# Moving the 64-row output jobs behind all wide jobs, with ten repeated transposes more, in an attention-plus-spectral-mix kernel

## The chip, the core and the metric

The kernel runs on one core of a Trainium2 chip. The metric is the device time of one execution in microseconds; a figure quoted for a kernel is the median of its runs. Spans and times inside a span come from the profile, whose zero is the first counted work; a span is some 2 us shorter than the timed run.

## The reference, cut to what matters

```python
def _attn_ref(q, k, v, f):                     # B, H, S, D = 8, 8, 576, 64
    scores = scale * q @ k^T + (cum[i] - cum[j])   # cum = cumsum(log f), causal
    return softmax(scores) @ v

def _moe_ref(x, w_r, w_i, w_ch):               # x: (8, 576, 512), 64 modes
    X = np.fft.rfft(x, axis=1)
    Y[:, :64] = einsum(X[:, :64], w_r + i w_i)     # one 512x512 matrix per mode
    u = x + np.fft.irfft(Y, n=S, axis=1)
    return u + np.maximum(u @ w_ch, 0.0)       # out: (8, 576, 512) float32
```

The output has 8 x 576 x 512 x 4 bytes = 9.44 MB. 576 rows are four blocks of 128 and one of 64 for each of the 8 batches; the 64-row blocks are what the change moves.

## The kernel before

Attention and transforms run while GpSimd's queue loads q, k, v and 64 + 64 weight matrices. After the last weights a tail is left, in which each job makes up to 256 rows of output: TensorE sums `u` and `z` (two PSUM tiles), ScalarE copies `u`, VectorE computes `max(z, 0) + u`, and SyncE issues the write. The list of jobs before:

```python
jobs = []
for b in range(0, B, 2):
    if b == 0:
        jobs += [((c, sb), (c, sb + 1)) for c in (b, b + 1) for sb in (0, 2)]
    else:
        jobs += [((b, sb), (b + 1, sb)) for sb in range(4)]     # wide jobs
    jobs.append(((b, 4),))                                      # a 64-row job: two batches
```

Sixteen jobs make 256 rows each: twelve of them, called wide, take 128 rows from each of two batches, and the four of batches 0 and 1 take 256 rows of one. Four are 64-row jobs. The writes:

```python
def emit_o(job, ps, u, o, pair, split=False):
    ...
        nc.vector.scalar_tensor_tensor(
            o[:, bs, :], ps[1][:, bs, :], 0.0, u[:, bs, :], ALU.max, ALU.add
        )
        if sb == 4:                      # 64 rows of batch b and 64 of batch b + 1
            for h in range(2):
                nc.sync.dma_start(
                    out[b + h, 512:576, :], o[64 * h : 64 * h + 64, 0, :]
                )
        ...
        elif sb % 2 or n_wide < 2:       # a pair of wide jobs: two writes of 512 KB
            ...                          # (the first two wide jobs are written singly)
                nc.sync.dma_start(
                    out[bj, 128 * (sb - sb % 2) :, :][0:256, :].rearrange(
                        "(p r) e -> p r e", r=2
                    )[:, rs, :],
                    pair[:, j, rs, :],
                )
```

The repeated transposes are in the attention stage. They do no useful work; they only add instructions:

```python
VREP = range(16, 25)
...
for sc in [0] * (5 if s in VREP else 0) + list(range(NSB)):
    nc.tensor.transpose(vp[:, sc, :, :]..., VTs[...][:, h, sc * 128 : (sc + 1) * 128], ident_bf)
```

The softmax here doesn't subtract the row's maximum and nothing guards it: scores larger than these inputs give would overflow.

## Time and profile before

| | before |
|---|---|
| time | 436.08 us, median of 3 (436.05 to 436.23) |
| span of the profile | 434.3 us |
| last weights land, last weight matmuls | 399.3, 399.38 us |
| output arithmetic of VectorE | 403.1 to 426.2 us |
| last output packet | 432.6 us |
| last block of TensorE instructions fetched | 425.1 us, 0.92 us on one DMA engine |

Two tools go below the printed lines. The first is a table by windows: for each stretch of the span, the busy time of every engine, the granted TensorE clock, the busy share of the 16 DMA engines and GB/s. The second is the trace's packet records, read by a script, as no view prints them: every DMA packet with its start, duration, size and queue, but not the DMA engine that carried it. Below, *tail* means the time from the start of the last weight matmul to the end of the span: 434.28 - 399.57 = 34.7 us here.

### The profile page before, as it was taken

To read this page: it belongs to the slowest core of one execution; us is meant where nothing else is said; L and a number is where in the kernel's file an instruction comes from. 1 tells how busy PE (TensorE), PEld (TensorE's weight loads), DVE (VectorE), ACT (ScalarE), POOL (GpSimd) and SP (SyncE) were. 2 spreads that over 40 slices of the span, in tenths; PEclk is the share of its full clock that TensorE was granted. 3 is DMA by queue.
4 is the path that set the end of the run, shared out by engine and by line. 5 is a ranking of instruction groups with operands and counts; after the bars stand their busy time and mean duration, and the time that the engine had idled before them with its cause. 6 is when DMAs were issued, how large, how long until landed. Compare 5 with 4: busy or idle time off the path is not lost.

```text
span 434.3 us, 12369 instructions
## 1 busy us (share of the span) xinstructions
PE 358.8 (83%) x5328; PEld 247.5 (57%) x5346; DVE 264.4 (61%) x659; ACT 225.0 (52%) x339; POOL 126.8 (29%) x198
## 2 busy tenths in 40 slices
PE   3787799999987978878778797799999977888881
PEld 2454566776665756666656565666665544554540
DVE  5797888876465665556566577524324654653892
ACT  2888488774526446364464554143443443731771
POOL 8333332223232232332323322232222322200400
PEclk9996899996557868577597779599999999999997
DMA  8999999999999999999999999999999999996697
GB/s 181 235 235 239 236 237 238 246 212 217 228 220 237 220 229 233 215 237 227 222 236 212 213 211 211 211 211 211 211 211 211 211 211 211 211 212 127 240 383 272
DMA packets 51086, 97.39 MB, mean 224 GB/s; under 512 B 3799, under 2 KB 12983, under 8 KB 51031
## 3 DMA queue, kind: packets, MB, share of 16 engines
q0 software_dynamic: 46464, 85.65, 101.0%
q1 hardware_dynamic: 4567, 10.95, 7.1%
q8 instruction: 42, 0.69, 0.6%
q14 instruction: 13, 0.11, 0.1%
HBM read 163.73 MB, written 9.44 MB: 399 GB/s over the span
## 4 chain that ended last, share of the span: by engine, by line
PE 33%; DMA 27%; ACT 11%; DVE 11%; issue 5%; DVEq 0%; POOL 0%; ACTq 0%; SPq 0%
DMA wb<-in_moe_w_i_dram 26%; ACT E L590 8%; PE pav L628 7%; PE A L191 6%; PE ps L583 6%; PE tp L321 5%; PE vp L555 3%; PE px L671 2%; DVE QTs L336 2%; ACT KT L334 2%; DVE x_all L650 1%; DVE os L1019 1%; PE pz L842 1%; DVE XT L685 1%; DVE E L605 1%
## 5 line engine op out<-in xcount | busy, mean ns | idle before, releaser
L590 ACT ACTIVATE E<-ps 128x1024 bf16<-128x1024 f32 (+1 forms) x128 | 101.3, 849 | 28.2 <-PE pav L628 17.2
L191 PE MATMUL A<-XT,wb 128*128 128x16 bf16 x1984 | 71.9, 181 | 12.0 <-DMA wb<-in_moe_w_i_dram 7.0
L191 PEld LDWEIGHTS <-wb 128*128 128x128 bf16 x1984 | 64.1, 100 | 27.5 <-issue 13.2
L96 POOL DMA_DIRECT2D wb<-in_moe_w_r_dram x64 | 42.7, 667 | 123.6 <-PE A L191 24.7
L583 PE MATMUL ps<-QTs,KT 64*128 64x64 bf16 (+4 forms) x384 | 55.8, 320 | 14.5 <-ACT E L590 12.4
L96 POOL DMA_DIRECT2D wb<-in_moe_w_i_dram x64 | 42.3, 660 | 81.7 <-DMA wb<-in_moe_w_i_dram 38.1
L628 PE MATMUL pav<-va,E 128*128 128x65 bf16 (+1 forms) x1088 | 53.6, 205 | 7.1 <-DVE x_all L650 6.5
L628 PEld LDWEIGHTS <-E 128*128 128x128 bf16 (+1 forms) x1088 | 43.6, 111 | 17.2 <-DVE x_all L650 8.9
L605 DVE TENSOR_TENSOR E<-E,trimask 128x256 bf16<-128x256 bf16 (+2 forms) x128 | 37.0, 304 | 19.5 <-ACT E L590 18.8
L881 ACT CAST XW<-pxw 128x512 bf16<-128x512 f32 x36 | 20.7, 587 | 35.6 <-PE pxw L874 23.4
L340 ACT COPY VT<-tp 128x640 bf16<-128x640 bf16 (+1 forms) x32 | 23.1, 759 | 28.3 <-PE tp L321 28.3
L583 PEld LDWEIGHTS <-KT 64*128 64x128 bf16 x384 | 19.1, 99 | 31.4 <-issue 20.8
L334 ACT COPY KT<-tp 128x640 bf16<-128x640 bf16 (+1 forms) x32 | 22.0, 751 | 26.0 <-PE tp L321 25.8
L924 ACT CAST XW<-pB 128x512 bf16<-128x512 f32 x36 | 21.1, 586 | 26.7 <-PE pB L842 26.6
L874 PE MATMUL pxw<-wch,yy 128*128 128x512 bf16 x133 | 33.6, 385 | 1.1 <-issue 0.5
L923 DVE CAST x_all<-pA 128x512 bf16<-128x512 f32 x36 | 24.9, 692 | 12.5 <-PE pA L842 10.6
L336 DVE COPY QTs<-tp 128x640 bf16<-128x640 bf16 (+1 forms) x32 | 23.4, 768 | 14.2 <-PE tp L321 14.0
L650 DVE TENSOR_TENSOR x_all<-pav,rcp 128x384 bf16<-128x384 f32 x64 | 29.1, 455 | 1.1
L639 DVE RECIPROCAL rcp<-pav 128x6 f32<-128x6 f32 x64 | 12.1, 189 | 24.5 <-PE pav L628 23.6
L156 DVE TENSOR_TENSOR YTe<-A,Yacc 128x128 bf16<-128x128 f32 x16 | 5.9, 368 | 33.1 <-PE A L191 33.1
L555 PE MATMUL vp<-ident_bf,VT 128*128 128x128 bf16 x205 | 21.4, 256 | 4.5 <-DVE QTs L336 3.8
L842 PEld LDWEIGHTS <-ident_bf 64*64 64x64 bf16 (+1 forms) x336 | 15.1, 107 | 17.0 <-issue 8.2
(142 smaller groups left out, 610.8 us busy)
## 6 DMA issues: line engine op xcount, KB each, us to landing
wb<-in_moe_w_r_dram POOLq DMA_DIRECT2D x62, 512.0 KB, 16.7
wb<-in_moe_w_i_dram POOLq DMA_DIRECT2D x62, 512.0 KB, 17.4
stv<-in_v_dram POOLq DMA_DIRECT2D x9, 576.0 KB, 15.6
out_dram<-os SPq DMA_DIRECT2D x10, 512.0 KB, 4.8
stk<-in_k_dram POOLq DMA_DIRECT2D x11, 288.0 KB, 15.6
stq<-in_q_dram POOLq DMA_DIRECT2D x11, 288.0 KB, 15.4
wx<-in_v_dram POOLq DMA_DIRECT2D x5, 576.0 KB, 16.2
out_dram<-uo SPq DMA_DIRECT2D x3, 512.0 KB, 4.2
```

The source lines that it names most:

```text
L96: keep(nc.gpsimd.dma_start(dst, src))
L191: ins = nc.tensor.matmul(A[:, eb, mi, :], lhsT=w_of(mi, eb * 128), rhs=x_of(m), start=(i == 0), stop=(i == len(terms) - 1),)
L334: nc.scalar.copy(rows(KTs[pr % 2][:, :, 0:S]), tv)
L336: ins = nc.vector.tensor_copy(rows(QT[pr][:, :, :]), tv)
L555: nc.tensor.transpose(vp[:, sc, :, :].rearrange("p b d -> p (b d)"), VTs[s // 2 % 2][:, h, sc * 128 : (sc + 1) * 128], ident_bf[:, :],)
L583: nc.tensor.matmul(ps[:, b, o : o + n], lhsT=KTs[pr % 2][bs, h, jb * 128 : (jb + 1) * 128], rhs=QT[pr][bs, h, jb * 128 + c0 : jb * 128 + c ...
L590: nc.scalar.activation(E[:, :, piece * 512 : piece * 512 + w], ps[:, :, 0:w], ACT.Exp, scale=scale,)
L605: nc.vector.tensor_tensor(dg, dg, tr, ALU.mult)
L628: nc.tensor.matmul(pav[64 * half : 64 * half + w, slot, :], lhsT=E[:, b, c : c + (w - 1) * st + 1 : st], rhs=va[:, jb, b, :], start=(n == ...
L650: nc.vector.tensor_tensor(xo, pi, ri, ALU.mult)
L874: nc.tensor.matmul(pxw[:, :], lhsT=xT[:, eb, i * 128 : (i + 1) * 128], rhs=wch[:, eb, :], start=(eb == 0), stop=(eb == NDC - 1),)
L923: nc.vector.tensor_copy(xs, pA[:, :])
```

## The change

The intent: 64-row jobs no longer stand between wide jobs but follow them all, and ten more transposes in the attention stage move the points at which TensorE fetches its instructions.

```diff
-    VREP = range(16, 25)
+    VREP = range(16, 27)
...
                 jobs += [((b, sb), (b + 1, sb)) for sb in range(4)]
-            jobs.append(((b, 4),))
+        jobs += [((b, 4),) for b in range(0, B, 2)]
```

## The prediction

> **What bounds the kernel now.** I read the page first, then the chain of waits in order of time, then a table of the last 35 us by windows, then SyncE's own queue. The page says how the DMA engines stand over the whole span (40 slices of 10.86 us) and what the queues carried:
>
> ```profile
> span 434.3 us, 12369 instructions
> ...
> DMA  8999999999999999999999999999999999996697
> ...
> q0 software_dynamic: 46464, 85.65, 101.0%
> q1 hardware_dynamic: 4567, 10.95, 7.1%
> q8 instruction: 42, 0.69, 0.6%
> ```
>
> From the second slice to the 36th the DMA row shows 9: the loads of q, k, v and the weights are one unbroken stream. No TensorE work of that stage sets the end unless it starves the stream. The median weight load takes 16.7 us from issue to landing (part 6 of the page), so some 16 us of transfers stand queued at any time. The chain in order of time shows where the stream ends and the tail begins:
>
> ```profile
> 384.11 15.23 DMA wb<-in_moe_w_i_dram
> ...
> 414.97 1.24 DVE os L1019
> ...
> 416.29 3.23 DMA out_dram<-uo
> ...
> 425.18 0.41 DVE os L1019
> ```
>
> The last weights land at 399.3. All that the reordering touches lies behind it: 434.3 - 399.3 = 35.0 us. Windows of that tail (time, then busy us of PE, PEld, DVE, ACT and POOL, granted clock, DMA share, GB/s):
>
> ```profile
> 408.60:412.90 4.30, 3.84 (x64) 2.18 (x67) 3.91 (x4) 3.00 (x4) 0.00 (x0) 1.00 0.93 332
> 412.90:418.60 5.70, 4.78 (x78) 2.72 (x74) 5.31 (x6) 4.44 (x5) 0.00 (x0) 1.00 1.00 369
> 418.60:424.30 5.70, 4.78 (x74) 2.51 (x67) 5.31 (x6) 4.44 (x5) 0.00 (x0) 1.00 1.02 393
> 424.30:427.50 3.20, 0.75 (x6) 0.13 (x3) 1.88 (x3) 0.59 (x1) 0.00 (x0) 1.00 0.99 361
> 427.50:430.10 2.60, 0.00 (x0) 0.00 (x0) 0.00 (x0) 0.00 (x0) 0.00 (x0) 0.74 1.02 410
> 430.10:434.30 4.20, 0.00 (x0) 0.00 (x0) 0.00 (x0) 0.00 (x0) 0.00 (x0) 0.50 0.34 102
> ```
>
> Two things are nearly equal here. VectorE is busy 5.31 of the 5.70 us of a group (four wide jobs and one 64-row job). The DMA share is 1.00 from 412.9 on and stays there for 4 us after the last arithmetic (426.2). So the output DMA, not VectorE, has the last word. SyncE's issues at the end:
>
> ```profile
> 421.26 2.54 SPq L1026 DMA_DIRECT2D out_dram<-uo  x2
> 423.90 3.52 SPq L1039 DMA_DIRECT2D out_dram<-os  x4
> 427.54 2.48 SPq L1026 DMA_DIRECT2D out_dram<-uo  x2
> ```
>
> The two writes of a 64-row job (128 KB each) hold the queue 2.5 us; four writes of wide jobs (512 KB each) hold it 3.5 us. The last arithmetic ends at 426.2, its writes start issuing only at 427.5 and finish issuing at 430.0; the data flows until about 432.
>
> **What the Trainium skill says.** "DMA: Bandwidth & Descriptors", section "The descriptor swizzle", gives partitions 0-63 to the even SBUF ports and 64-127 to the odd ones. A 64-row write reads from one half only, so half of the ports can serve it. The trace agrees in part: its packet records show 2 KB packets of 64-row writes taking 113 to 136 ns in the windows in which they dominate against 85 to 86 ns for the 2 KB packets of wide writes, and the rate falls from 410 GB/s to 186-268 GB/s around 411.5, 418.3, 424.3 and 430.5. "Perfetto Trace Analysis", section "Per-instruction lifecycle", says that the profiled time of such an issue is lock wait and descriptor generation, without the movement. The trace shows one and the same kind of issue at 0.33 to 1.18 us (wide) and 0.54 to 1.48 us (64 rows), which I read as waiting for room behind earlier writes. "Runtime: NRT & Kernel Launch", section "Instruction fetch mechanics", has instructions fetched in blocks of 16 KiB, 256 instructions each. Queue 8 agrees: 42 packets, 0.69 MB, 16,384 bytes each, 0.9 to 1.0 us on one of the 16 DMA engines. The last ones start at 393.3, 401.3, 413.4 and 425.1.
>
> **The change part by part.**
>
> *Ten more transposes.* Two more attention steps repeat five transposes each. A run of ten such transposes lasts 1.22 us in the chain where a run of five lasts 0.69, so five more cost 0.53 us, ten 1.06 us of TensorE, around 165 to 180 us. The weight queue is some 16 us deep, so the load stream does not notice: 0 us on the end. They put 20 instructions (ten weight loads, ten matmuls) ahead of everything later. Each fetch comes 20 instructions earlier in the program, at some 0.05 us an instruction in the tail about a microsecond. The fetch of 401.3 would start near 400.4, still behind the last weights. That of 425.1 would start about 424. A fetch costs its engine about 0.9 us while the others go on, which fits the straggling packets after 431.75 (1.5 us with under a tenth of the engines busy). Moving it earlier does not remove it: 0 to -0.4 us.
>
> *Three 64-row jobs leave the gaps between wide jobs.* VectorE: each 64-row job takes 0.68 us, and two gaps of about 0.2 us stand around it (the waits for ScalarE's copy and "issue"). Without them the wide jobs follow each other at about 1.13 us, the spacing that three in 3.48 us show. Twelve wide jobs from 408.7 then end near 422.4 in place of 424.2-425.6, and the four 64-row jobs at 0.8 to 0.9 us each end near 425.8, against 426.2. Gain 0.4 us, but not at the end, as writes are behind.
>
> *Writes.* All 9.44 MB are the same. From 407.75, when the engines are first full, some 8.69 MB remain (9.44 less 0.75 that the packet records show before). Of these 6.59 MB go as 4 KB packets at 410 GB/s, 16.1 us; 1.05 MB as 2 KB packets of the first two wide jobs at 370 GB/s, 2.8 us; 1.05 MB as 64-row writes. In the kernel before, a 64-row job costs 0.26 MB / 410 = 0.64 us plus a loss of about 0.42 us, read from the two windows with dips (453 and 433 KB moved in 1.5 us where 615 would have been): 1.06 us, four of them 4.2 us. The sum is 23.1 us, so 430.9, and the records show the bulk ending about 431.5; the rest is the starving around 411-412 (rate 186 GB/s, share 0.71), where the first 64-row job held SyncE. The change removes that: the first wide write can be issued near 410 in place of 411.28. Gain 0.3 to 0.6 us.
>
> *What is given back.* Behind all wide jobs four 64-row jobs write alone, with no wide packets to fill the other half of the ports. At about 215 GB/s, 1.05 MB take 4.9 us in place of 4.2: +0.6.
>
> Sum: -0.45 (starving) -0.2 (VectorE, straggler; mostly hidden) +0.6 (half the ports) -0.4 (the last write to wait for is 128 KB, and no 1 MB pair stands in front of it) = about -0.45 us. 436.08 becomes 435.6.
>
> **The rivals.** (1) *SyncE becomes the bound.* If the 2.5 us for two 64-row writes is their own cost, not waiting for room, the four jobs take 4 x 2.5 = 10 us from about 423.6, so 433.6 for the last issue against 430.0: +3 us, 439. For it: every 64-row pair took over 2 us, whatever came before. Against it: the first write of the first job took 0.54 us, and wide issues also stretch to 1.18 us. I give it one in ten. (2) *Latency-bound 64-row writes.* If only about three writes may be outstanding, each 128 KB, and each needs about 2.2 us, the last megabyte runs at 175 GB/s and takes 6 us: +1 us net, 437. One in five. (3) *Full rate.* If writes of the two halves overlap, all 64-row data go near 400 GB/s and the end comes at about 434.7. One in five. (4) *The fetch shift disturbs the stream*: a fetch that falls before 399.3 would delay one engine's weights by 0.9 us, 436.8. The fetch has about a microsecond of room; one in ten.
>
> **Range and chances.** The middle is -0.45 us; rival 3 sets the lower edge at 434.6, rivals 2 and 4 the upper at 437.0, rival 1 lies outside. 2% is 8.7 us, a quarter of the whole tail, beyond any of these: faster 0.01, same 0.98, slower 0.01.
>
> **What would show it.** The last weights should land at 399.3 within 0.3 us. VectorE's wide jobs should run unbroken, 1.13 us apart, ending by 422.5. The dip in the output rate near 411-412 should be gone, and one long stretch near 215 GB/s should stand at the end. 64-row issues should shorten to about 0.6 us once the wide writes have drained; if they stay at 1.0 to 1.5 us with the engines idle, rival 1 is right and I am wrong. If the last weights land later, the fetch part is wrong.

## The result

435.81 us (435.36 to 436.12, six runs) against 436.06 us for the kernel before in the same rounds (435.78 to 436.84). The ratio is 0.9991, 95% interval 0.9978 to 1.0004: same, within the predicted range, and by itself not clear of noise. In a later set of rounds the changed kernel had 435.58 against 436.47, ratio 0.9982 (0.9970 to 0.9995).

The page of the changed kernel, the rows that answer to those shown of before:

```profile
span 434.1 us, 12383 instructions
...
DMA  8999999999999999999999999999999999996798
...
q1 hardware_dynamic: 4567, 10.95, 7.2%
q8 instruction: 42, 0.69, 0.6%
```

The stream of loads is as full as before. The same number of blocks is fetched. The tail by windows, with the same columns as in the prediction (time, busy us of PE, PEld, DVE, ACT, POOL, clock, DMA share, GB/s):

```profile
408.60:413.50 4.90, 4.19 (x67) 2.13 (x64) 4.88 (x5) 4.05 (x4) 0.00 (x0) 1.00 1.02 391
413.50:414.50 1.00, 0.93 (x20) 0.53 (x16) 1.00 (x2) 0.89 (x1) 0.00 (x0) 1.00 0.55 201
414.50:422.80 8.30, 7.77 (x108) 3.58 (x104) 8.30 (x9) 7.38 (x9) 0.00 (x0) 1.00 1.03 406
422.80:427.30 4.50, 1.85 (x18) 0.64 (x15) 2.55 (x4) 1.17 (x2) 0.00 (x0) 0.91 1.02 403
427.30:432.30 5.00, 0.00 (x0) 0.00 (x0) 0.00 (x0) 0.00 (x0) 0.00 (x0) 0.50 0.91 223
432.30:434.10 1.80, 0.00 (x0) 0.00 (x0) 0.00 (x0) 0.00 (x0) 0.00 (x0) 0.50 0.03 7
```

The three dips around 64-row writes are gone from the middle. VectorE is busy all the time up to 422.8. At the end stands one stretch of 5.0 us at 223 GB/s, in which only 64-row writes move, and it ends sharply. But a hole of one microsecond at 201 GB/s is there at 413.5. VectorE's wide jobs and SyncE's issues, from the timeline (start, length, engine, line, instruction, count):

```profile
408.86 13.91 DVE L1019 SCALAR_TENSOR_TENSOR os<-pz,us 128x1024 f32<-128x1024 f32 x12
...
410.10 14.59 SPq L1039 DMA_DIRECT2D out_dram<-os  x14
424.79 6.25 SPq L1026 DMA_DIRECT2D out_dram<-uo  x8
427.26 3.77 SPq L1026 DMA_DIRECT2D out_dram<-uo  x6
```

Twelve wide jobs take 13.91 us, 1.16 us each, without a gap. The eight 64-row writes are issued in 6.25 us; the last six of them, issued once the wide data had mostly drained, take 3.77 us, 0.63 us each with the gaps, where each pair of before took 2.1 to 2.5 us. The chain of waits, in order of time, differs in one place ahead of the tail:

```profile
383.85 0.91 PE A L191 x30
...
399.88 0.29 PE A L175 x8
...
424.99 0.69 DVE uo L1019
```

From 383.85 to the last weight matmuls it is TensorE that holds the path, not the loads: those matmuls come at 399.8, 0.43 us later than before (399.38), although the packet records put the last weight packet at 398.6, against 398.8 before. The reason is in the granted clock between 384 and 390 us (changed kernel, then the kernel before):

```profile
384.00:390.00 6.00, 5.95 (x61) 3.00 (x60) 2.81 (x5) 1.76 (x3) 0.53 (x1) 0.72 1.12 211
```

```profile
384.00:390.00 6.00, 5.86 (x97) 3.76 (x98) 3.03 (x6) 2.35 (x4) 0.53 (x1) 1.00 1.12 211
```

At a clock of 0.72 TensorE did 61 recorded matmuls where it did 97 before. So of the tail's gain, 34.7 - 34.1 = 0.65 us, this profile gave 0.43 us away again before the tail began. Whether that belongs to the change was the first thing to test.

### The profile page after: what moved, and what is told of

It reads as the page before. It is cut to its first block, busy times and chain, and to the rows that moved or that the text cites. A ratio compares the mean times of both kernels' runs of the same rounds, so it can differ in the third digit from the quotient of the medians.

```text
span 434.1 us, 12383 instructions
## 1 busy us (share of the span) xinstructions
PE 360.6 (83%) x5338; PEld 249.1 (57%) x5356; DVE 263.5 (61%) x659; ACT 225.5 (52%) x339; POOL 126.9 (29%) x198
## 4 chain that ended last, share of the span: by engine, by line
DMA 36%; PE 30%; ACT 9%; DVE 8%; issue 4%; POOL 0%; ACTq 0%; DVEq 0%
DMA wb<-in_moe_w_i_dram 36%; ACT E L590 7%; PE pav L628 6%; PE A L191 5%; PE tp L321 5%; PE ps L583 4%; PE vp L555 2%; PE pu L842 2%; DVE QTs L336 2%; ACT KT L334 2%; PE px L671 1%; PE pz L842 1%; DVE os L1019 1%; DVE x_all L650 1%; DVE E L605 1%
## 5 line engine op out<-in xcount | busy, mean ns | idle before, releaser
L583 PE MATMUL ps<-QTs,KT 64*128 64x64 bf16 (+4 forms) x384 | 53.7, 312 | 14.6 <-ACT E L590 12.4
L881 ACT CAST XW<-pxw 128x512 bf16<-128x512 f32 x36 | 20.7, 587 | 34.8 <-PE pxw L874 23.4
L340 ACT COPY VT<-tp 128x640 bf16<-128x640 bf16 (+1 forms) x32 | 23.3, 759 | 28.8 <-PE tp L321 28.7
L924 ACT CAST XW<-pB 128x512 bf16<-128x512 f32 x36 | 20.9, 586 | 29.8 <-PE pB L842 29.7
L874 PE MATMUL pxw<-wch,yy 128*128 128x512 bf16 x133 | 32.9, 379 | 1.1 <-issue 0.5
```

What stands on the lines that cost most here:

```text
L583: nc.tensor.matmul(ps[:, b, o : o + n], lhsT=KTs[pr % 2][bs, h, jb * 128 : (jb + 1) * 128], rhs=QT[pr][bs, h, jb * 128 + c0 : jb * 128 + c ...
L874: nc.tensor.matmul(pxw[:, :], lhsT=xT[:, eb, i * 128 : (i + 1) * 128], rhs=wch[:, eb, :], start=(eb == 0), stop=(eb == NDC - 1),)
```

## The experiments

Twelve runs were made, three of them repeats (e3, e9, e13); each has five timed executions, e7 four. A table first; the tail is read from each run's own profile. Rows between lines shared a chip and the runs of the kernel before.

| run | time us | before us | ratio (95%) | tail us |
|---|---|---|---|---|
| before, first profile | 436.08 | | | 34.7 |
| changed kernel, first | 435.81 | 436.06 | 0.9991 (0.9978 to 1.0004) | 34.1 |
| --- | | | | |
| e1 reordering only | 435.79 | 436.47 | 0.9989 (0.9976 to 1.0003) | 34.0 |
| e2 transposes only | 435.93 | 436.47 | 0.9989 (0.9976 to 1.0001) | 33.9 |
| e3 changed kernel again | 435.58 | 436.47 | 0.9982 (0.9970 to 0.9995) | 34.0 |
| e4 second half on ScalarE's queue | 436.03 | 436.47 | 0.9992 (0.9980 to 1.0005) | 34.4 |
| --- | | | | |
| e6 one write, wrong rows | 434.73 | 436.20 | 0.9965 (0.9953 to 0.9978) | 32.9 |
| e7 one write from GpSimd | 442.78 | 436.20 | 1.0152 (1.0138 to 1.0165) | 41.5 |
| e8 ten transposes fewer | 437.08 | 436.20 | 1.0022 (1.0008 to 1.0035) | 35.0 |
| e9 before again | 436.49 | 436.20 | 1.0008 (0.9996 to 1.0021) | 34.8 |
| --- | | | | |
| e10 interleaved rows | 434.94 | 436.25 | 0.9965 (0.9952 to 0.9979) | 33.1 |
| e11 the same, old order | 435.02 | 436.25 | 0.9974 (0.9958 to 0.9991) | 33.4 |
| --- | | | | |
| e12 interleaved, 20 instructions fewer | 435.39 | 436.87 | 0.9964 (0.9951 to 0.9976) | 33.2 |
| e13 e10 again | 435.07 | 436.87 | 0.9958 (0.9944 to 0.9971) | 33.0 |

The tail, from one profile a run, repeats much better than the time: 34.7 and 34.8 for the kernel before, 34.1 and 34.0 for the changed one, 33.1 and 33.0 for e10 and e13, while single runs of one kernel spread over a microsecond. Differences under half a microsecond are therefore read from tails.

My theory going in was that the reordering makes the gain in the stream of writes, and that the transposes do nearly nothing. The rival was the reverse.

### e1: the reordering alone

```diff
-    VREP = range(16, 27)
+    VREP = range(16, 25)        # in the changed kernel
```

> The reordering alone, with nine steps of repeated transposes as before. Theory A (the gain is made by the write stream behind the last weights): time 0.2 to 0.6 us under the kernel before; the tail from the last weight matmuls to the end about 33.9 us as in the changed kernel (34.6 before); VectorE's twelve wide jobs unbroken, about 13.9 us; 64-row stretch near 215 GB/s at the end. Rival B (the ten transposes and the shifted fetches make the gain): time equal to before within 0.15 us, or slower, and packets straggling at the end as before. Rival C (only the granted clock differs between profiles): no difference in the tail either.

Measured: tail 34.0 us, as in the changed kernel; 435.79 against 436.47. The reordering by itself is enough for the shorter tail. The clock between 384 and 390 us was 0.72 again and the last weight matmuls came at 399.8 again, here without the transposes.

### e2: the transposes alone

```diff
-    VREP = range(16, 25)
+    VREP = range(16, 27)        # in the kernel before
```

> The ten transposes alone, jobs in the order of before. Theory A: within 0.15 us of before, the last weights land at about the same time, the tail 34.6 us as before, with the same three dips of the output rate around the 64-row writes. Rival B: 0.2 to 0.6 us faster, and the straggling packets at the end gone. A slowing of 0.3 us or more would say that the longer attention stage reaches the end after all.

Measured: a miss for my theory. In the old order the ten transposes alone shorten the tail to 33.9 us, and the time is 435.93 against 436.47. The dips of the output rate are as before. VectorE's arithmetic keeps its place (from first to last 23.06 us, before 23.04); only the data ends sooner after it started: the last output packet comes 28.7 us after the first output arithmetic, 29.5 in the kernel before. What differs most plainly is the last fetch of instructions: at 423.1 us in place of 425.1. It is not alone: the fetch before it moved too (413.4 to 412.2), and with 2 MB still to write e2 is already 0.3 us ahead, counted from the first output arithmetic (22.95 us, before 23.25). Each part alone gives 0.7 to 0.8 us of tail, and together they give 0.65: the two gains do not add.

### e3: the changed kernel again

> The changed kernel once more, to have it in the same rounds as its two parts. Theory A: equal to the reordering alone within 0.2 us, 0.2 to 0.6 us under before. Its profile may or may not show the low granted clock of 0.72 at 384 to 390 us that the first profile of it showed; if the clock is 1.00 there, the last weight matmuls should come near 399.4 as before (they came at 399.9) and the span fall by up to 0.4 us. Rival: the late last weight matmuls belong to the change itself and come again at 399.9 with the clock at 1.00.

Measured: 435.58 us, tail 34.0. This time the clock stayed at 1.00 between 384 and 390, and the last weight matmuls came at 399.03:

```profile
384.00:390.00 6.00, 5.89 (x90) 3.59 (x89) 3.14 (x6) 2.34 (x4) 0.36 (x1) 1.00 1.13 212
```

The rival is refuted: the late weight matmuls of the first profile are not a property of the change. The span was 433.3 us here. This clock can explain a part of the spread between runs, not all of it: in e2 it was 1.00, and the last weights themselves landed late (the last matmuls waited for them until 399.79).

### e4: the two halves side by side

```diff
-    nc.sync.dma_start(
+    (nc.sync, nc.scalar)[h].dma_start(
         out[b + h, 512:576, :], o[64 * h : 64 * h + 64, 0, :]
```

> The changed kernel, but the second of the two 128 KB writes of each 64-row job is issued from ScalarE's queue, so that rows from partitions 0-63 and 64-127 move side by side. Theory (each write alone can use only one half of the SBUF ports): the last megabyte moves at 350 to 400 GB/s in place of 215, the packets of 2 KB take 85 to 100 ns in place of 131 to 147, and the end comes 1 to 2 us earlier than in the changed kernel: ratio to before near 0.995. Rival (64-row writes are slow for another reason: their own size, or the receiving memory): still 200 to 250 GB/s, and the time within 0.3 us of the changed kernel. Rival 2: ScalarE waits in its queue behind VectorE before each write and holds up the copies of the following 64-row jobs; then the arithmetic ends later than 425.7 and the gain shrinks.

Measured: 436.03 us, tail 34.4: no gain. The rates show why (windows of e4, the last two are after most of the arithmetic):

```profile
421.00:425.50 4.50, 3.78 (x40) 1.32 (x30) 3.79 (x5) 2.79 (x5) 0.00 (x0) 1.00 1.03 401
425.50:427.50 2.00, 0.00 (x0) 0.00 (x0) 0.69 (x1) 0.19 (x1) 0.00 (x0) 1.00 1.01 315
427.50:432.00 4.50, 0.00 (x0) 0.00 (x0) 0.00 (x0) 0.00 (x0) 0.00 (x0) 0.74 0.92 306
```

Side by side the end runs at 306 GB/s in place of 223. Wide packets are in this window until 429.9; from 430 to 431, with 64-row packets of both queues alone, it is 309 GB/s, and a 2 KB packet takes 95 ns on average in place of 135. But the writes from partitions 64-127 no longer wait behind the wide writes; they run beside them and slow those to 315 GB/s from 425.5 on. The low rate begins two microseconds sooner and is less deep. The last packet comes 28.7 us after the first output arithmetic (28.8 in the changed kernel), but the span ends 2.17 us after it (1.71): the extra 0.4 us of tail lies behind the data. The second rival came true too: ScalarE's last copy was held up and the arithmetic ended at 426.4 instead of 425.7. The run speaks for a limit in each half, as its writes still have 128 KB each, but the rate stayed under the 350 GB/s that I had expected.

### e6: one write from all partitions

```diff
-    for h in range(2):
-        nc.sync.dma_start(
-            out[b + h, 512:576, :], o[64 * h : 64 * h + 64, 0, :]
-        )
+    one = out[b, 512, :]
+    nc.sync.dma_start(
+        bass.AP(tensor=one.tensor, offset=one.offset,
+                ap=[[D, 64], [S * D, 2], [1, D]]),
+        o[:, 0, :],
+    )
```

> The changed kernel with one write of 256 KB per 64-row job in place of two of 128 KB: all 128 partitions at once, row r of the two batches taken from partitions 2r and 2r+1. The values land in wrong rows on purpose; bytes, target region and arithmetic are the same. Theory (half of the SBUF ports limits a 64-row write): the last megabyte moves at 370 to 410 GB/s in place of 215 (packets of 2 KB at 85 to 95 ns in place of 131 to 147), it takes some 2.7 us in place of 5, and the tail from the last weight matmuls to the end falls from 34.0 to about 31.8 to 32.5 us, 1.5 us or more off the time. Rival (the small contiguous target region or the packet size is slow): still 215 to 250 GB/s and a tail of 34 us.

Measured: 434.73 us against 436.20, tail 32.9 (wrong rows). The window in which the 64-row data moves:

```profile
427.60:430.20 2.60, 0.00 (x0) 0.00 (x0) 0.00 (x0) 0.00 (x0) 0.00 (x0) 0.87 1.02 386
430.20:433.00 2.80, 0.00 (x0) 0.00 (x0) 0.00 (x0) 0.00 (x0) 0.00 (x0) 0.50 0.08 31
```

386 GB/s against 223, with the same bytes in packets of the same 2 KB to the same target regions. A packet takes 86 ns on average in place of 135. The rival (small packets, or the region in memory) is refuted: what made the 64-row writes slow is that each read from one half of the partitions. One write of 256 KB instead of two of 128 KB was part of the edit, so the size of a write was not separated here; against it as the cause stand the 309 GB/s and 95 ns of e4, whose writes have 128 KB. The issues, at 0.5 to 0.8 us each once the wide data had drained, were not the limit in either case. The tail stayed 0.4 us above what I had expected, because a few packets trail behind the bulk (the second line); more on these under e8 and e9.

### e7: one write in the right rows, from GpSimd

```diff
+    nc.gpsimd.dma_start(
+        bass.AP(tensor=one.tensor, offset=one.offset,
+                ap=[[S * D, 2], [D, 64], [1, D]]),
+        o[:, 0, :],
+    )
```

> The changed kernel with one write of 256 KB per 64-row job from all 128 partitions, issued from GpSimd's queue, rows where they belong (correct result). If that write is spread over all 16 engines by partition, the last megabyte moves at 350 GB/s or more and the tail falls by 1 to 2 us as in the run with wrong rows. If it is spread over few engines because the outer dimension of the target is 2, the rate falls far under 215 GB/s and the time rises by several us.

Measured: 442.78 us, the second case of the expectation. The windows after the wide writes:

```profile
428.00:434.00 6.00, 0.00 (x0) 0.00 (x0) 0.00 (x0) 0.00 (x0) 0.00 (x0) 0.50 0.52 124
434.00:441.20 7.20, 0.00 (x0) 0.00 (x0) 0.00 (x0) 0.00 (x0) 0.00 (x0) 0.50 0.17 45
```

A share of 0.17 of 16 engines is fewer than three. I put this down to the target's outer dimension of 2, where e6 has 64 outside and 2 inside. That is argued, not separated: the edit also changed the queue, and with it the packets (4 KB, with many of 8 bytes between them, in place of 2 KB). GpSimd's queue as such can keep the engines busy: the weight loads on it have a share of 1.12.

### e8 and e9: ten transposes fewer, and the kernel before again

```diff
-    VREP = range(16, 25)
+    VREP = range(16, 23)        # e8, in the kernel before; e9 has no edit
```

> The order of before with ten repeated transposes fewer than before, 20 instructions, so that the last block of instructions, fetched at 425.1 in before while the last writes move, begins behind the program's end or later. Theory (that fetch holds one DMA engine 0.9 us, and its late packets set the end of the kernel before): if the fetch is gone, the tail is 33.9 to 34.1 us as with ten transposes more, and 0.3 to 0.7 us of the time go; if it comes later instead, at 426 or after, the stragglers are as in before or worse, 34.7 us or more. Rival (ten transposes more helped in another way, or the difference was noise of single profiles): 34.7 us as before although the fetch is gone.

> The kernel before once more, to see what its profile repeats. Theory: fetch near 425.1 again, a few late packets after the bulk of the output again, and 34.6 to 34.8 us from the last weight matmuls to the end; time equal to before within 0.2 us. If the tail comes out at 34.0 us, the difference of the tails that I read between single profiles is not to be trusted.

Measured: e9 repeats the kernel before (tail 34.8, last fetch at 425.3). In e8 the fetch did not vanish; it came later, at 426.0, and the tail is 35.0 us, the second case of the expectation. The time, 437.08 against 436.20, is clearly slower, the only such case among the runs that differ in transposes alone. Not all of that is the tail: the clock of this profile was 0.72 between 384 and 390 us again, and the last weight matmuls came at 399.7. The same window of one microsecond, 431.5 to 432.5, for before, e2 and e8:

```profile
431.50:432.50 1.00, 0.00 (x0) 0.00 (x0) 0.00 (x0) 0.00 (x0) 0.00 (x0) 0.50 0.14 51
```

```profile
431.50:432.50 1.00, 0.00 (x0) 0.00 (x0) 0.00 (x0) 0.00 (x0) 0.00 (x0) 0.50 0.11 39
```

```profile
431.50:432.50 1.00, 0.00 (x0) 0.00 (x0) 0.00 (x0) 0.00 (x0) 0.00 (x0) 0.50 0.48 164
```

In these spans output arithmetic began at 403.1 (before), 403.5 (e2) and 403.5 (e8), so e2 is further along at the same distance from its start. Counted from that beginning, the last packet comes 29.5 us later in before, 29.6 in e9, 28.7 in e2 and 29.7 in e8, with the last fetch at 425.1, 425.3, 423.1 and 426.0.

This is the pattern that I take from it. A fetch holds one DMA engine (0.9 to 1.3 us for the last one, up to 1.8 us for earlier ones in the tail) and leaves its share of the writes late. A late engine can catch up while all the others are held back by a 64-row write. In e2 the fetch falls just ahead of the third dip (424 to 425.5); in before, e9 and e8 it falls as that dip ends or behind it, and only wide writes and one last 64-row job follow. In the new order every fetch of the tail has the 5 us stretch at 223 GB/s (the slow stretch) behind it, so there its place does not matter: the last packets come 28.8 us after the first output arithmetic in e1 (fetch at 425.1), in the changed kernel (422.7) and in e3 (421.9).

How much of this is shown can be read from the end of the packet records: the time from the first output arithmetic until 50 KB are left to write, and the time that these last 50 KB take.

| run | until 50 KB are left, us | the last 50 KB, us |
|---|---|---|
| before, e9 | 28.5, 28.7 | 1.1, 0.9 |
| changed kernel, e1, e3 | 28.6, 28.6, 28.7 | 0.3, 0.2, 0.2 |
| e6, e10, e13 (new order, no slow stretch) | 26.8, 26.8, 26.7 | 1.2, 1.4, 1.4 |
| e2, e8 (old order, transposes changed) | 28.0, 28.5 | 0.8, 1.3 |

In before mostly one or two packets are in flight while the last 50 KB move. Up to there the changed kernel is not ahead of before; its whole gain lies in the last 50 KB. Where the slow stretch is taken away (e6, e10, e13), the trailing packets are back. So it is shown that the slow stretch at the end hides packets that otherwise trail. That the last fetch makes them trail fits, but is inferred: the records do not name the engine, and e11 (below), with no fetch after 414.4, still takes 0.8 us for its last 50 KB. In the old order the trailing packets account for 0.3 of the 0.8 us of e2. In e8 they account for most of the 0.3 us lost, but there VectorE's arithmetic also ran 0.5 us longer (23.6 us), as TensorE waited until 405.0 for a copy of `yy`. With one profile each and other fetches moved as well, the effect of the last fetch's place is suggested by e2 and e8, not shown.

### e10 and e11: the right rows, in both orders

e6 can be made correct: the matmuls can put row r of batch b + k on partition 2r + k. Two permuted unit matrices and two scattered basis tables (in the space of a table that is no longer needed) take the place of 64x64 blocks, and a job has four matmuls of 128x128 instead of eight of 64x64.

```diff
+    perm = [BI[:, 128 * t : 128 * t + 128] for t in range(2)]
+    BIp = [BI[:, 256 + 128 * t : 384 + 128 * t] for t in range(2)]
+    for t in range(2):
+        nc.vector.memset(BIp[t][:, :], 0.0)
+        for k in range(2):
+            hf = k ^ t
+            nc.vector.tensor_copy(
+                _strided(perm[t][:, k : k + 1], [[2, HM]]), ident_bf[:, HS[hf]])
+            nc.vector.tensor_copy(
+                _strided(BIp[t][HS[hf], k : k + 1], [[2, HM]]), BIl[HS[hf], 512:576])
...
+    if len(job) == 1:                         # in terms()
+        b, sb = job[0]
+        p = ps[t][:, 0, :]
+        rows = [
+            [(p, perm[t][:, :], (x_all, XW)[t][:, b // 2, xi(b, sb), :], True)],
+            [(p, BIp[t][:, :], yy[:, 1, b // 2, t, :], False)],
+        ]
+        return [r for k, r in enumerate(rows) if "xy"[k] in what]
...                                            # and the write of e6
```

> The changed kernel with a correct form of the write from all 128 partitions: the rows of the two batches of a 64-row job are brought to partitions 2r and 2r+1 by the matmuls themselves (two permuted unit matrices and two scattered basis tables, 128 rows each, in place of 64x64 blocks), so four matmuls a job in place of eight, and one write of 256 KB. Theory: as with the wrong rows, 385 to 395 GB/s in the last megabyte, a tail of 32.9 us from the last weight matmuls, time 1.2 to 1.8 us under before. Rival: the full-width matmuls or the write's dims (64 by 2) cost something that the run with wrong rows did not show; then the tail is 33.5 us or more.

> The same write and matmuls in the order of before, 64-row jobs between the wide ones, nine steps of repeated transposes. If the half of the ports was all that made a 64-row job dear, the three dips of the output rate go, and this order is as good as the other: tail 32.9 to 33.4 us, time within 0.3 us of the run in the new order. If the place of the 64-row jobs matters by itself (VectorE's gaps around each, SyncE held up), the new order stays 0.3 us or more ahead.

Measured: both are correct. e10 takes 434.94 us against 436.25, tail 33.1, and the 64-row data moves at 388 GB/s:

```profile
428.10:430.70 2.60, 0.00 (x0) 0.00 (x0) 0.00 (x0) 0.00 (x0) 0.00 (x0) 1.00 1.02 388
430.70:433.80 3.10, 0.00 (x0) 0.00 (x0) 0.00 (x0) 0.00 (x0) 0.00 (x0) 0.51 0.08 28
```

e11, the old order, takes 435.02, tail 33.4. With writes that use all partitions the dips that the 64-row writes made are gone in either order, and the place of the 64-row jobs is worth 0.3 us of tail at most, within the noise of the times (e11 also has the nine steps of transposes, as e12 has: 33.2). What remains in both is a hole at 414.5 us, of half a microsecond in e10 and a whole one in e11, just before the first pair of wide jobs is written.

### e12 and e13: the late fetch once more

```diff
-    VREP = range(16, 27)
+    VREP = range(16, 25)        # e12, in e10; e13 is e10 without an edit
```

> The interleaved 64-row jobs in the new order, with nine steps of repeated transposes in place of eleven, 20 instructions fewer. The four-matmul jobs have 32 instructions fewer than before, and in the old order the last fetch of instructions, at 423 to 425 us elsewhere, was then gone. Theory (that fetch makes one DMA engine late, and nothing behind it catches up once the 64-row writes run at full rate): the fetch is gone here too, the packets after the bulk shrink from 1.3 us to 0.7 or less, tail 32.3 to 32.7 us against 33.1 with it, time 0.3 to 0.7 us under the same kernel with the fetch. Rival (late packets have another cause): tail 33.1 us.

> The interleaved kernel with eleven steps of repeated transposes again, in the same rounds: last fetch near 423 us, a tail of 32.9 to 33.2 us from the last weight matmuls, late packets for about 1.3 us after the bulk; time 1.1 to 1.6 us under before.

Measured: e13 repeats e10 (435.07 against 436.87, tail 33.0). e12 is inconclusive: I had counted matmuls and weight loads alone, and the fetch was not gone but at 425.0. Tail 33.2, no gain. So what a tail of e10 without any late fetch would take stays open; e11, whose last fetch came at 414.4, still had trailing packets, but fewer: 0.8 us for the last 50 KB, against 1.3 in e12 and 1.4 in e10 and e13. e10 (with its repeat e13) is the best version: ratios 0.9965 and 0.9958, 1.3 and 1.8 us by the medians, against 0.9991 and 0.9982 for the change itself.

## Why the prediction was right, and where not

The total was right: 435.81 against 435.6, inside the range, and so was the claim that everything happens in the tail of 35 us. Its terms fared as follows.

- **The loads.** Right: the ten transposes left the stream full; the DMA row has a 9 in the same slices. The last weight packet moved from 398.8 to 398.6, within the 0.3 us of the prediction. The matmuls on the last weights came 0.43 us later, through the granted clock of 0.72, which came without the transposes in e1 and stayed away in e3. The fetch at 401.3 moved to 400.6, behind the weights, so rival 4 did not happen.
- **VectorE.** Right in mechanism, nearly in size: 1.16 us a wide job instead of 1.13, the last one ending at 422.8 instead of 422.4.
- **Half of the ports.** Right: 5.0 us at 223 GB/s, predicted 4.9 at 215; e6 takes the cause away and has 386 GB/s. Rival 3 (the halves overlap) is refuted for one queue; with two queues, e4, the rate rises to 309 GB/s but the end gains nothing.
- **SyncE's issues.** Right: most of their time was waiting, not their own cost. Rival 1 is refuted by the last six issues in 3.77 us, 0.63 us each once the wide data had drained; rival 2 (175 GB/s, 6 us) by 223 GB/s and 5.0 us.
- **"The change removes that" (starving around 411-412, 0.3 to 0.6 us).** This step failed. The first wide write was issued at 410.1 as predicted, but the hole came back at 413.5 to 414.5 (201 GB/s, share 0.55), ahead of the first pair, for which two wide jobs must be done. It is there in e1, in e3 (from 413) and in e10 as well, and in the old order e2 (414 to 415, 174 GB/s) and e9 (415 to 416, 252 GB/s) have one beside the dip at 411.
- **"The last write to wait for is 128 KB" (-0.4 us).** This did not show: from the start of the last packet to the end of the span it is 1.67 us before and 1.71 after.
- **The fetch and the straggler ("0 to -0.4 us", put into the sum as a part of -0.2).** Mis-sized, and it is the term that carried the result. The changed kernel is level with before until 50 KB are left, and writes these in 0.3 us in place of 1.1. The prediction had it come from the moved fetch; e1 has the same gain with the fetch at 425.1, so it is the reordering, with its slow stretch at the end, that gives it. "About a microsecond" for the shift of the fetch was too little (425.1 to 422.7), and the 1.5 us of straggling reach past the last packet, which starts at 432.6. That the transposes alone also shorten the tail, and that the two parts do not add, was not in the prediction.

So the sum was right partly by luck: two credits of 0.3 to 0.6 and 0.4 us that did not come stood for one of 0.7 to 0.8 that I had put at 0.2.

## What to carry to other kernels

Where the last thing a kernel does is write, look at which partitions each write reads: here one that takes 64 of 128 partitions moved at little more than half the rate, and having the matmuls interleave the rows, so that one write covers all partitions with a long outer dimension, was worth more than any order of the jobs. When two small edits each give a gain and together no more, ask what single thing both repair. Read effects of half a microsecond from a stretch of the trace that repeats to 0.1 us, not from times that spread over one.

## What the Trainium skill lacked or had wrong

- "DMA: Bandwidth & Descriptors", section "Rules for kernel authors", says of two transfers to disjoint partition halves that they serialize, and to use one 128-partition transfer. The advice held (e6, e10: 386 and 388 GB/s); but for two writes on two queues the rate did rise here, from 223 to 309 GB/s (e4). That an outer dimension of 2 confines a write to few engines agrees with e7 (45 GB/s at the end), where the queue was changed too.
- "Runtime: NRT & Kernel Launch", section "Instruction fetch mechanics", calls the cost of a block boundary mostly hidden. But a fetch takes 0.9 to 1.8 us of one DMA engine in these tails, and the end of a write-bound kernel moved along with it: 0.8 us less tail with the last fetch 2.0 us earlier (e2), 0.2 to 0.3 us more with it 0.9 us later (e8). That the fetch is the cause is not shown.
- No page that I read says how long an issue on SyncE's queue stretches behind earlier writes: the 128 KB writes took 0.53 us to issue at the shortest and 1.25 us behind wide writes in the changed kernel. That they wait for room is my reading of this.
